# The steps of a long convolution, put on TensorE as row tiles and column tiles instead of zero-padded full-size products

## The chip, the cores and the metric

The kernel runs on one core of one Trainium2 chip. The metric is the device time of one execution in microseconds (us). The kernel before takes 2110.37 us, the median of three runs (2103.78 to 2110.42).

## The reference: what is computed

The program computes a layer and its gradients. The input is normalized over its 1024 channels, then goes into two branches: branch A, a long convolution along the 2048 positions for each channel, and branch B, a gated MLP of width 3584.

```
xn = layernorm(x)
# branch A: q = xn
k_shift[t] = sum over i<4 of k[t-i] * shift_k[i]          # four taps per channel
kv = k_shift * v
y  = irfft(rfft(kv, padded to 4096) * rfft(ssm_k, padded to 4096))[:2048] + kv * ssm_D
A  = xn * y
# branch B
h  = relu(xn @ W_gate) * (xn @ W_up);   B = h @ W_down
out = x + A + B
# then jax.vjp: the gradients of out for x, k, v, shift_k, ssm_k, ssm_D, W_gate, W_up, W_down
```

All tensors are bf16. The ten outputs are `out` and nine gradients.

## The kernel before, in words

**Branch B** (class `LnMlp`) is a chain of large matrix products of 128 x 128 weights by 512 columns: `hidden` (up, gate and the gradient of the hidden layer; L573), `grad_down` and `grad_in` (weight gradients; L670), then `out_phase` (L754) and `grad_x` (L787). ScalarE (ACT) and VectorE (DVE) take its results out of the accumulators, and all its stores and loads go through SyncE's queue (SP).

**Branch A** (class `ABranch`) works on eight groups of 128 channels, one after the other (`steps`). The 2048 positions are split in stages, so that each Fourier transform becomes small matrix products. For one group:

- `h_tile`: 16 transposes on TensorE turn the filter `ssm_k` so that positions lie on partitions (`pst`); DVE copies the result to `hT`.
- `fwd1` (three times: filter `hT`, gradient `gt`, signal `kvt`): four accumulators of two products each (weights `R`, 512 columns); ACT copies each to `B`; DVE's `flip` transposes `B` in blocks of 32.
- `fwd2` (three times): 32 products of 128 columns with the table `FW`; ACT writes `H`, `G`, `K`. `cmul` on DVE multiplies them pointwise.
- `inv_a` (three times) and `flip`: 32 products of 128 columns with the table `IA`.
- `inv_b` (for the gradient `gkv` and for `yt`): two accumulators of four products each with `RB`, 512 columns. `inv_b_chan` does the same for the gradient of the filter, with `RN`.
- `grad_taps`: 16 products of 512 columns accumulate, for every pair of channels in the group, the product of `gks` and `kp`; only the diagonal is used (DVE multiplies by the identity, `dg`, and sums).
- `gradients` on DVE: `gv`, `gks`, `gk`. A DMA `gks<-gks` copies the three first rows of each partition to the partition before, as the taps need them.

Before the change a partition holds 16 neighbouring positions (`tview`: partition q, row r). `R` has 128 rows, of which every second one is zero for each parity `u` of q; `RB` has 128 columns, of which every second one is zero for each `u`, and the two parities are summed in the accumulator.

**Order of the work.** Both branches are written as generators. Each `yield` of branch A gives a budget in nanoseconds, which the steps of branch B use up, so that steps of A are put between products of B. Every instruction carries a priority (`Pri.now`, or `Pri.late` for ACT, DVE and stores), and a planner then writes a fixed list for each engine by these priorities and by when it thinks that operands are ready. An engine works off its list in order. So the list of a queue, once written, decides who waits behind whom. Branch A has small pools: two accumulators (`aps`), three time tiles (`ts`), and one buffer each for `kp`, `vt` and `ksh` (`a_lng`): `kp` of the next group is loaded only when `grad_taps` of this group has read it.

Of the kernel before, what the change touches and what calls it, by code (L numbers as in the profile page):

```python
# [17 lines left out]
P = 128  # L18
# [21 lines left out]
NB1 = 32  # L40


class ABranch:

# [57 lines left out]
    def tables(self):  # L102
# [6 lines left out]
        self.R = con.tile([P, 2, 2, 2, NB1], BF16, name="R")  # L109
        self.RB = con.tile([P, 2, NB1, 2, 2], BF16, name="RB")  # L110
        self.RN = con.tile([P, NB1, 2], BF16, name="RN")
# [23 lines left out]
        n1 = pbit(124, 0.25, "n1p")  # L135
        nh = pbit(2, 0.5, "nhp")
        up = pbit(1, 1.0, "up")
# [10 lines left out]
        nu = lin(up, -1.0, 1.0, "nu")  # L148
        nnh = lin(nh, -1.0, 1.0, "nnh")
        for u, mu in ((0, nu), (1, up)):  # L150
            for n2h, mh in ((0, nnh), (1, nh)):
                V.tensor_scalar(out=self.R[:, u, n2h, :, :], in0=tr[:], scalar1=mu[:], scalar2=mh[:],
                                op0=ALU.mult, op1=ALU.mult)
# [42 lines left out]
        V.memset(self.RB[:], 0.0)  # L196
        nb64 = lin(b64, -1.0, 1.0, "nb64")
        for n2h, mh in ((0, nb64), (1, b64)):
            for o in (self.RB[:, 0, :, n2h, 0], self.RB[:, 1, :, n2h, 1], self.RN[:, :, n2h]):
                V.tensor_scalar(out=o, in0=trB[:], scalar1=mh[:], scalar2=1.0 / 2048, op0=ALU.mult, op1=ALU.mult)  # L200

        make_identity(nc, self.identA[:])
        sk_b = con.tile([P, self.NG * 4], BF16, name="sk_b")
# [8 lines left out]
    def tview(self, ap2d, cg):  # L212
        return ap2d[:, cg].rearrange("(q r) c -> q r c", r=16)
# [4 lines left out]
    def loads_1(self, gi):  # L218
# [4 lines left out]
        self.load(gt[:], self.tview(self.g, cg))  # L223
        xv = self.tview(self.xn_d, cg)
        xt = self.tmp.tile([P, 16, P], BF16, name="xt", tag="tmp")
        self.load(xt[:], xv)
# [5 lines left out]
    def loads_2(self, st):  # L232
# [8 lines left out]
        self.load(vt[:], self.tview(self.v, cg))  # L241
# [14 lines left out]
    def h_tile(self, st):  # L256
        hn = st["hn"]
        hT = self.ttile("hT")
        hv = hn[:].rearrange("p r c -> p (r c)").rearrange("p (q r) -> p r q", r=16)
        pst = self.ps.tile([P, 16, P], BF16, name="pst", tag="aps")  # L260
        for r in range(16):
            self.pri.now()
            self.nc.tensor.transpose(pst[:, r, :], hv[:, r, :], self.identA[:])
        self.vcopy(hT[:, 0:16, :], pst[:])
        return hT

    def flip(self, src):
# [3 lines left out]
        sf = src[:].rearrange("p cp r i -> p (cp r i)").bitcast(F32).rearrange("p (cp r) -> p cp r", cp=64)  # L271
# [5 lines left out]
    def fwd1(self, src, ns, add_D=None):  # L277
        B = self.big.tile([P, 64, NB1, 2], BF16, name="B", tag="big")
        for u in range(2):
            for j in range(2):  # L280
                ps = self.ps.tile([P, 1024], F32, name="ps1", tag="aps")
                for jj in range(2):
                    r0 = 8 * j + 4 * jj
                    self.mm(ps[:, 512 * jj:512 * jj + 512], self.R[:, u].rearrange("p h a k -> p (h a k)"),
                            src[:, r0:r0 + 4, :].rearrange("p r c -> p (r c)"))
                t0 = 16 * u + 8 * j
                self.act(B[:, :, t0:t0 + 8, :], ps[:].rearrange("p (r cp i) -> p cp r i", r=8, i=2))
                if add_D is not None and t0 == 0:
                    b0 = B[0:NB1, :, 0, :]
                    self.tt(b0, b0, add_D[:].rearrange("p (cp i) -> p cp i", i=2), ALU.add)  # L290
                if u + j == 2:
                    self.flipped = self.flip(B)
                yield ns
# [32 lines left out]
    def inv_a(self, Q, ns):  # L326
        C = self.big.tile([P, 64, NB1, 2], BF16, name="C", tag="big")
        for k0 in range(0, NB1, 8):
# [4 lines left out]
            if k0 == NB1 - 8:  # L333
                self.flipped = self.flip(C)
# [13 lines left out]
    def inv_b_chan(self, Cf, dst, ns):  # L348
        dv = dst[:, 0:16, :].rearrange("p r c -> p (r c)").rearrange("p (q n) -> p q n", n=NB1)
        for n0 in range(0, NB1, 16):  # L350
            ps = self.ps.tile([P, 16, 64], F32, name="ps5", tag="aps")
            for j in range(16):
                self.mm(ps[:, j, :], Cf[:, n0 + j, :], self.RN[:].rearrange("p n h -> p (n h)"))
# [3 lines left out]
    def grad_taps(self, gi, gks, kp, ns):  # L357

        ps = self.ps.tile([P, 4, P], F32, name="ps6", tag="aps")
        for r in range(16):  # L360
            self.mm(ps[:].rearrange("p b c -> p (b c)"), gks[:, r, :], kp[:, r:r + 4, :].rearrange("p b c -> p (b c)"),
                    start=(r == 0), stop=(r == 15))
            if r % 4 == 3:
                if r == 15:
                    dg = self.tmp.tile([P, 4, P], F32, name="dg", tag="tmp")
                    self.tt(dg[:], ps[:], self.identA[:].rearrange("p (o c) -> p o c", o=1).to_broadcast([P, 4, P]),
                            ALU.mult)
                    self.pri.late()
                    self.nc.vector.tensor_reduce(out=self.gs_all[:, gi, :], in_=dg[:], axis=AX.X, op=ALU.add)
                yield ns  # L370

    def steps(self):
# [4 lines left out]
        for gi in range(self.NG):  # L377
# [39 lines left out]
            self.store(self.tview(self.y_d, cg), yt[:, 0:16, :])  # L417
# [498 lines left out]
```

## Time and profile before

| what | before |
|---|---|
| median of three runs | 2110.37 us |
| the profiled execution's own time | 2113.93 us |
| its span | 2112.2 us |
| granted TensorE clock, mean | 0.978 |
| TensorE products (PE) busy | 1983.0 us, 94% |
| VectorE (DVE) busy | 1003.4 us, 48% |
| ScalarE (ACT) busy | 693.2 us, 33% |
| end of branch A's last products | about 1310 us from the start |

A row of a group reads: line, engine, operation, output<-inputs, shape and count, then busy us, mean ns of one, and the engine's idle time just before with what ended it. A row of the timeline reads: start, length, engine, line, operation, count, and in brackets the idle time before it and its releaser. A product's length in these rows reaches from its start to its modelled end; the spacing of products in a stream is shorter, and is read from two starts.

### The profile page before, as it was taken

To read this page: it belongs to the slowest core of one execution; us is meant where nothing else is said; L and a number is where in the kernel's file an instruction comes from. 1 tells how busy PE (TensorE), PEld (TensorE's weight loads), DVE (VectorE), ACT (ScalarE), POOL (GpSimd) and SP (SyncE) were. 2 spreads that over 40 slices of the span, in tenths; PEclk is the share of its full clock that TensorE was granted. 3 is DMA by queue.
4 is the path that set the end of the run, shared out by engine and by line. 5 is a ranking of instruction groups with operands and counts; after the bars stand their busy time and mean duration, and the time that the engine had idled before them with its cause. 6 is when DMAs were issued, how large, how long until landed. Compare 5 with 4: busy or idle time off the path is not lost.

```text
span 2112.2 us, 26202 instructions
## 1 busy us (share of the span) xinstructions
PE 1983.0 (94%) x10502; PEld 947.0 (45%) x10502; DVE 1003.4 (48%) x1450; ACT 693.2 (33%) x902; POOL 20.1 (1%) x46
## 2 busy tenths in 40 slices
PE   3799989889999998989999899999998999999998
PEld 2345435445444544535445454444443444444443
DVE  4848667666865954746557574000011213232232
ACT  6455337337436535537365373111100000000000
POOL 2000000000000000000000000000000000000000
PEclk9899999989999999999999999999998999999999
DMA  9764565965466474352473425933499745544551
GB/s 259 191 162 120 156 173 138 211 156 145 118 166 176 143 210 126 102 147 93 133 218 107 134 71 162 313 116 116 105 249 241 185 120 131 126 110 110 127 122 53
DMA packets 614811, 319.03 MB, mean 151 GB/s; under 512 B 448800, under 2 KB 583968, under 8 KB 614688
## 3 DMA queue, kind: packets, MB, share of 16 engines
q1 hardware_dynamic: 613408, 313.15, 55.7%
q0 software_dynamic: 1280, 4.20, 0.6%
q8 instruction: 82, 1.34, 0.3%
q14 instruction: 41, 0.34, 0.1%
HBM read 141.36 MB, written 95.44 MB: 112 GB/s over the span
## 4 chain that ended last, share of the span: by engine, by line
PE 78%; DVE 7%; DMA 7%; ACT 4%; issue 2%; SPq 1%; DVEq 0%; POOL 0%; ACTq 0%
PE ps_x L787 18%; PE ps_w L670 16%; PE ps_o L754 9%; PE ps L64 7%; PE ps_u L573 7%; PE ps_g L573 7%; PE ps_h L573 7%; PE ps_d L670 6%; DMA kp<-in_A_k_dram 3%; DVE tap L72 1%; ACT H L68 1%; ACT G L68 1%; DMA gks<-gks 1%; DVE ksh L72 1%; DVE flp L274 1%
## 5 line engine op out<-in xcount | busy, mean ns | idle before, releaser
L670 PE MATMUL ps_w<-ugs,xn_nat 128*128 128x512 bf16 x1792 | 403.0, 380 | 5.1 <-DMA xn_nat<-xn_d 5.1
L573 PEld LDWEIGHTS <-xnT 128*128 128x128 bf16 x1792 | 174.7, 99 | 210.4 <-issue 19.9
L670 PEld LDWEIGHTS <-xn_nat 128*128 128x128 bf16 x1792 | 173.4, 98 | 206.4 <-DMA xn_nat<-xn_d 5.8
L573 PE MATMUL ps_h<-wdT,goT 128*128 128x512 bf16 x896 | 213.7, 385 | 13.9 <-DVE ru L631 11.7
L573 PE MATMUL ps_g<-wg,xnT 128*128 128x512 bf16 x896 | 214.1, 389 | 5.4 <-DVE ru L631 5.4
L670 PE MATMUL ps_d<-g_nat,hs 128*128 128x512 bf16 x896 | 212.9, 386 | 4.0 <-DMA g_nat<-in_grad_out_dram 4.0
L573 PE MATMUL ps_u<-wu,xnT 128*128 128x512 bf16 x896 | 209.8, 381 | 1.4 <-DMA wu<-in_B_W_up_dram 1.2
L754 PE MATMUL ps_o<-wd,hT 128*128 128x512 bf16 x896 | 199.5, 387 | 8.0 <-DMA hT<-h_d 8.0
L787 PE MATMUL ps_x<-wuT,guT 128*128 128x512 bf16 x896 | 198.6, 379 | 0.0
L787 PE MATMUL ps_x<-wgT,ggT 128*128 128x512 bf16 x896 | 198.6, 379 | 0.0
L756 DVE TENSOR_TENSOR o<-ps_o,ya 128x512 bf16<-128x512 f32 x32 | 21.5, 687 | 263.5 <-PE ps_o L754 263.5
L754 PEld LDWEIGHTS <-hT 128*128 128x128 bf16 x896 | 88.9, 99 | 118.4 <-DMA hT<-h_d 9.2
L708 ACT CAST wi<-ps_w 128x512 bf16<-128x512 f32 x112 | 65.5, 586 | 229.8 <-PE ps_w L670 226.7
L643 ACT CAST gh<-ps_h 128x512 bf16<-128x512 f32 x112 | 65.5, 585 | 228.3 <-PE ps_h L573 119.4
L573 PEld LDWEIGHTS <-goT 128*128 128x128 bf16 x896 | 87.0, 99 | 113.5 <-issue 21.2
L787 PEld LDWEIGHTS <-ggT 128*128 128x128 bf16 x896 | 87.7, 98 | 105.7
L787 PEld LDWEIGHTS <-guT 128*128 128x128 bf16 x896 | 87.7, 98 | 105.7
L274 DVE STREAM_TRANSPOSE flp<-B 128x1024 f32<-128x1024 f32 x48 | 89.8, 1938 | 93.9 <-ACT B L68 93.9
L670 PEld LDWEIGHTS <-hs 128*128 128x128 bf16 x896 | 86.9, 99 | 103.4 <-issue 12.6
L789 DVE CUSTOM_DVE_ANT_0 gx<-ps_x,gy 128x512 f32<-128x512 f32 x32 | 22.1, 692 | 223.2 <-PE ps_x L787 223.2
L68 ACT CAST B<-ps 128x1024 bf16<-128x1024 f32 x96 | 96.2, 1016 | 76.5 <-PE ps L64 76.3
L68 ACT CAST C<-ps 128x1024 bf16<-128x1024 f32 x96 | 96.7, 1019 | 51.0 <-PE ps L64 51.0
(159 smaller groups left out, 1769.9 us busy)
## 6 DMA issues: line engine op xcount, KB each, us to landing
ug_d<-ru SPq DMA_DIRECT2D x112, 256.0 KB, 2.8
ugs<-ug_d SPq DMA_DIRECT2D x112, 256.0 KB, 4.8
wg<-in_B_W_gate_dram SPq DMA_DIRECT2D x56, 256.0 KB, 4.2
wu<-in_B_W_up_dram SPq DMA_DIRECT2D x56, 256.0 KB, 3.8
h_d<-ht SPq DMA_DIRECT2D x112, 128.0 KB, 2.0
hs<-h_d SPq DMA_DIRECT2D x56, 256.0 KB, 4.6
out_dram<-wi SPq DMA_DIRECT2D x56, 256.0 KB, 3.3
out_dram<-wo SPq DMA_DIRECT2D x28, 256.0 KB, 2.0
```

The costliest lines, as they stand in the source:

```text
L64: self.nc.tensor.matmul(out, lhsT=lhsT, rhs=rhs, start=start, stop=stop)
L68: self.nc.scalar.copy(out=out, in_=in_)
L72: self.nc.vector.tensor_tensor(out=out, in0=in0, in1=in1, op=op)
L274: self.nc.vector.transpose(out=df[:, c0:c0 + 32, :], in_=sf[:, c0:c0 + 32, :])
L573: self.nc.tensor.matmul(ps[:], lhsT=xT[:, kt * P:(kt + 1) * P], rhs=w(kt), start=(kt == 0), stop=(kt == self.DT - 1))
L643: nc.scalar.copy(out=gh[:], in_=ps[:])
L670: self.nc.tensor.matmul(ps[:], lhsT=lhsT(st), rhs=rhs(st), start=(st == 0), stop=(st == self.ST - 1))
L708: nc.scalar.copy(out=wo[:, d, :], in_=ps[:])
L754: nc.tensor.matmul(ps[:], lhsT=hT[:, kt, :], rhs=self.wd[:, kt, oc], start=(kt == 0), stop=(kt == self.FT - 1))
L756: nc.vector.tensor_tensor(out=o0[:, oc], in0=ps[:], in1=ya[:, oc], op=ALU.add)
L787: nc.tensor.matmul(ps[:], lhsT=T[:, kt, :], rhs=W[:, kt, oc], start=(i == 0), stop=(i == n - 1))
L789: V.tensor_tensor_reduce(out=gx[:, oc], in0=ps[:], in1=gy[:, oc], scale=1.0, scalar=0.0, op0=ALU.add, op1=ALU.add, accum_out=m[:, ob:ob + 1])
```

## The change

Positions are dealt out in another way: partition 64u + q holds row r of positions 32q + 16u + r, so that the parity `u` selects a half of the partitions. The padded zeros then go away:

- `fwd1`: `R` becomes a table of 64 rows for each half. A pair of products takes rows 0 to 63 and rows 64 to 127, each into its own 512-column half of the accumulator (two row tiles). There are as many products as before.
- `inv_b`: `RB` becomes 64 columns. The two products of a parity pair no longer accumulate; they write partitions 0 to 63 and 64 to 127 (two column tiles). There are as many products as before.
- `grad_taps`: each of the 16 products of 128 x 128 by 512 becomes four products of 32 channels by their own 32 channels and 4 shifts (128 columns) into four column tiles. 64 products in place of 16; the two DVE steps behind read 128 columns in place of 512. The generator yields once in place of four times.
- `h_tile`: each transpose becomes two with 64 columns of weights.
- Every load and store of a time tile is two DMAs of 64 partitions; so are the loads of `kp`'s three extra rows and the copy `gks<-gks`.

```diff
     def tview(self, ap2d, cg):
-        return ap2d[:, cg].rearrange("(q r) c -> q r c", r=16)
+        return ap2d[:, cg].rearrange("(q u r) c -> u q r c", u=2, r=16)
+
+    def load_time(self, t, ap2d, cg):
+        for u in range(2):
+            self.load(t[64 * u:64 * u + 64], self.tview(ap2d, cg)[u])
+
+    def store_time(self, ap2d, cg, t):
+        for u in range(2):
+            self.store(self.tview(ap2d, cg)[u], t[64 * u:64 * u + 64, 0:16, :])
...
-        self.load(kp[:, 3:19, :], kv)
-        self.load(kp[1:P, 0:3, :], kv[0:P - 1, 13:16, :])
+        self.load_time(kp[:, 3:19, :], self.k, cg)
+        self.load(kp[64:P, 0:3, :], kv[0, :, 13:16, :])
+        self.load(kp[1:64, 0:3, :], kv[1, 0:63, 13:16, :])
...
         for r in range(16):
-            self.pri.now()
-            self.nc.tensor.transpose(pst[:, r, :], hv[:, r, :], self.identA[:])
+            for u in range(2):
+                self.pri.now()
+                self.nc.tensor.transpose(pst[64 * u:64 * u + 64, r, :], hv[:, r, u, :], self.identA[:])
...
     def fwd1(self, src, ns, add_D=None):
...
+        for r0 in range(0, 16, 4):
+            ps = self.ps.tile([P, 2, 4, P], F32, name="ps1", tag="aps")
+            for u in range(2):
+                rows = slice(64 * u, 64 * u + 64)
+                self.mm(ps[:, u].rearrange("p r c -> p (r c)"), self.R[rows].rearrange("p h a k -> p (h a k)"),
+                        src[rows, r0:r0 + 4, :].rearrange("p r c -> p (r c)"))
+            self.act(B[:, :, :, r0:r0 + 4, :], ps[:].rearrange("p u r (cp i) -> p cp u r i", i=2))
...
     def inv_b(self, Cf, dst, ns):
...
-                    self.mm(ps[:, 512 * jj:512 * jj + 512], self.RB[:, u].rearrange("p n h u -> p (n h u)"),
-                            Cf[:, n0:n0 + 4, :].rearrange("p n c -> p (n c)"), start=u == 0, stop=u == 1)
+                    self.mm(ps[64 * u:64 * u + 64, 512 * jj:512 * jj + 512],
+                            self.RB[:].rearrange("p n h -> p (n h)"), Cf[:, n0:n0 + 4, :].rearrange("p n c -> p (n c)"))
...
     def grad_taps(self, gi, gks, kp, ns):
 
-        ps = self.ps.tile([P, 4, P], F32, name="ps6", tag="aps")
+        ps = self.ps.tile([P, 4, 32], F32, name="ps6", tag="aps")
         for r in range(16):
...
+            for b in range(0, P, 32):
+                self.mm(ps[b:b + 32], gks[:, r, b:b + 32], kp[:, r:r + 4, b:b + 32], start=(r == 0), stop=(r == 15))
+        dg = self.tmp.tile([P, 4, 32], F32, name="dg", tag="tmp")
+        self.tt(dg[:], ps[:], self.ident32[:].to_broadcast([P, 4, 32]), ALU.mult)
...
-        self.store(gks[0:P - 1, 16:19, :], gks[1:P, 0:3, :])
+        self.store(gks[0:64, 16:19, :], gks[64:P, 0:3, :])
+        self.store(gks[64:P - 1, 16:19, :], gks[1:64, 0:3, :])
```

**What moves in the lists.** The planner writes other lists, because tiles, DMAs and budgets have changed. Two places show it, both at the passage from the fifth group of channels to the sixth (call such a passage a seam; there are seven).

DVE before, at the end of the fifth group: `ksh<-kp` is the first step that reads the next group's `kp`, and `hT<-pst` is the copy that the next group's first `fwd1` reads.

```order
L72 TENSOR_TENSOR dg<-ps_8301,identA 128x512
L369 TENSOR_REDUCE gs_all<-dg 128x4
L76 COPY gD_all<-ghn 128x1
L72 TENSOR_TENSOR ksh<-kp,skb 128x2048
L72 TENSOR_TENSOR tap<-kp,skb 128x2048 x2
L72 TENSOR_TENSOR ksh<-ksh,tap 128x2048 x2
L76 COPY hT<-pst 128x2048
```

DVE in the changed kernel, at the same place:

```order
L73 TENSOR_TENSOR dg<-ps_8499,ident_443 128x128
L371 TENSOR_REDUCE gs_all<-dg 128x4
L77 COPY gD_all<-ghn 128x1
L77 COPY hT<-pst 128x2048
L73 TENSOR_TENSOR ksh<-kp,skb 128x2048
L73 TENSOR_TENSOR B<-B,sD 32x64x2
L73 TENSOR_TENSOR tap<-kp,skb 128x2048 x2
```

The copy to `hT` has moved ahead of the steps that read `kp`. It stands behind them in all seven seams before, and ahead of them in four of the seven now (first to second group, fourth to fifth, fifth to sixth, seventh to eighth).

SP before, at the same seam: `kp` is loaded by two DMAs that stand behind the store of `gk`, the result of DVE's last taps.

```order
L84 DMA gks<-gks 127x384
L84 DMA y_d<-yt 2048x1x128
L691 DMA out_dram<-wo 128x1024
L80 DMA skb<-sk_d 128x512
L84 DMA out_dram<-gk 2048x1x128
L80 DMA kp<-in_A_k_dram 128x16x128
L80 DMA kp<-in_A_k_dram 127x3x128
```

SP in the changed kernel:

```order
L85 DMA gks<-gks 64x384
L85 DMA gks<-gks 63x384
L694 DMA out_dram<-wo 128x1024
L85 DMA y_d<-yt 64x16x128
L85 DMA y_d<-yt 64x16x128
L81 DMA kp<-in_A_k_dram 64x16x128
L81 DMA kp<-in_A_k_dram 64x16x128
L81 DMA kp<-in_A_k_dram 64x3x128
L81 DMA kp<-in_A_k_dram 63x3x128
L81 DMA skb<-sk_d 128x512
```

The loads of `kp` have moved ahead of `skb` and of the store of `gk`, and the whole program has 72 more DMAs on SP (1084 against 1012).

On PE the tiled products stand between full-size ones. In the changed list there are 135 runs of tiled products (88 of row tiles in `fwd1`, 39 of 64-column tiles in `inv_b` and `h_tile`, 8 of 32-column tiles in `grad_taps`), so TensorE goes 270 times from one kind of product to the other. The 64 products of `grad_taps` stand in one run; before, its 16 stood in three or four runs with products of branch B between them. At the fifth seam 50 products of branch B now stand between `inv_b` and the third `inv_a`, where 8 stood; and 1 or 2 stand between the four tiles of that `inv_a`, where none or 8 stood.

More of the change, by code (lines that the diff above doesn't have):

```diff
@@ L277, in fwd1 @@
     def fwd1(self, src, ns, add_D=None):
[L278 to L293, printed above, removed]
+        B = self.big.tile([P, 64, 2, 16, 2], BF16, name="B", tag="big")
+        for r0 in range(0, 16, 4):
[5 more added lines that the diff above has]
+            self.act(B[:, :, :, r0:r0 + 4, :], ps[:].rearrange("p u r (cp i) -> p cp u r i", i=2))
+            if add_D is not None and r0 == 0:
+                b0 = B[0:NB1, :, 0, 0, :]
+                self.tt(b0, b0, add_D[:].rearrange("p (cp i) -> p cp i", i=2), ALU.add)
+            if r0 == 12:
+                self.flipped = self.flip(B[:].rearrange("p cp u r i -> p cp (u r) i"))
+            yield ns
     def fwd2(self, Bf, F, ns):
@@ L357, in grad_taps @@
     def grad_taps(self, gi, gks, kp, ns):
-        ps = self.ps.tile([P, 4, P], F32, name="ps6", tag="aps")
+        ps = self.ps.tile([P, 4, 32], F32, name="ps6", tag="aps")
         for r in range(16):
[L361 to L370, printed above, removed]
+            for b in range(0, P, 32):
+                self.mm(ps[b:b + 32], gks[:, r, b:b + 32], kp[:, r:r + 4, b:b + 32], start=(r == 0), stop=(r == 15))
+        dg = self.tmp.tile([P, 4, 32], F32, name="dg", tag="tmp")
+        self.tt(dg[:], ps[:], self.ident32[:].to_broadcast([P, 4, 32]), ALU.mult)
+        self.pri.late()
+        self.nc.vector.tensor_reduce(out=self.gs_all[:, gi, :], in_=dg[:], axis=AX.X, op=ALU.add)
+        yield ns
     def steps(self):
```

45 lines of the change are left out of this document (20 added, 25 removed).

## The prediction

> **What bounds the kernel now.** I read the page first, then the groups of TensorE, the waits of PE, and the timeline at the places where PE waits.
>
> ```profile
> span 2112.2 us, 26202 instructions
> PE 1983.0 (94%) x10502; PEld 947.0 (45%) x10502; DVE 1003.4 (48%) x1450; ACT 693.2 (33%) x902; POOL 20.1 (1%) x46
> PE 78%; DVE 7%; DMA 7%; ACT 4%; issue 2%; SPq 1%; DVEq 0%; POOL 0%; ACTq 0%
> ```
>
> PE is busy 94% of the span and holds 78% of the chain that ended last. Both other shares matter: while branch A runs, DVE and DMAs are links of that chain. So there are two places for a gain or a loss: the time that PE needs for branch A's products, and PE's waits at the seams between groups. Time taken from PE shortens the end almost one for one, since branch B's products follow at once on the same engine.
>
> The products that the change touches, and two ACT groups that empty accumulators:
>
> ```profile
> L64 PE MATMUL ps<-hT,R 128*128 128x512 bf16 x64 | 22.7, 440 | 34.7 <-DVE hT L76 34.7
> L64 PE MATMUL ps<-kvt,R 128*128 128x512 bf16 x64 | 18.9, 379 | 1.4 <-ACT H L68 1.4
> L64 PE MATMUL ps<-gt,R 128*128 128x512 bf16 x64 | 18.7, 379 | 0.0
> L64 PE MATMUL ps<-flp,RB 128*128 128x512 bf16 x128 | 32.7, 379 | 1.8 <-ACT C L68 1.8
> L64 PE MATMUL ps<-kp,gks 128*128 128x512 bf16 x128 | 32.2, 379 | 0.0
> L263 PE MATMUL pst<-identA,hn 128*128 128x128 bf16 x128 | 10.6, 236 | 0.0
> L64 PEld LDWEIGHTS <-RB 128*128 128x128 bf16 x128 | 12.5, 98 | 17.1 <-issue 2.1
> L68 ACT CAST C<-ps 128x1024 bf16<-128x1024 f32 x96 | 96.7, 1019 | 51.0 <-PE ps L64 51.0
> ```
>
> The busy sums hold each short run's last tail and are not what a product costs in a stream. That is read from starts:
>
> ```profile
> 95.35 3.62 PE L573 MATMUL ps_h<-wdT,goT 128*128 128x512 bf16 x16
> 98.80 3.62 PE L573 MATMUL ps_g<-wg,xnT 128*128 128x512 bf16 x16
> 303.99 0.59 PE L64 MATMUL ps<-gt,R 128*128 128x512 bf16 x2
> 304.42 1.89 PE L573 MATMUL ps_g<-wg,xnT 128*128 128x512 bf16 x8
> 314.35 0.61 PE L64 MATMUL ps<-flp,FW 128*128 128x128 bf16 x8
> 314.80 1.89 PE L573 MATMUL ps_h<-wdT,goT 128*128 128x512 bf16 x8
> 265.94 0.64 PE L64 MATMUL ps<-RN,flp 128*128 128x64 bf16 x16 [0.85 <-DVE flp L274]
> 266.41 1.89 PE L573 MATMUL ps_h<-wdT,goT 128*128 128x512 bf16 x8
> 925.17 1.16 PE L263 MATMUL pst<-identA,hn 128*128 128x128 bf16 x16
> 926.16 2.54 PE L670 MATMUL ps_d<-g_nat,hs 128*128 128x512 bf16 x11
> ```
>
> Sixteen products of 512 columns take 98.80 - 95.35 = 3.45 us, 216 ns each. A pair of `fwd1` takes 0.43 us, twice that: a pair of A between products of B costs nothing beside its columns. Eight products of 128 columns take 0.45 us, 56 ns each, sixteen of 64 columns 0.47 us, 29 ns each, sixteen transposes 0.99 us, 62 ns each; in all of them the weight load (98 ns) hides.
>
> **The tiles, term by term.**
>
> *fwd1.* 3 x 64 products in 96 pairs. If the halves run side by side, one of two costs nothing: 96 x 0.216 = -20.7 us. If they run one after the other, 0. *inv_b.* 128 products in 64 pairs: -13.8 us, or 0. *grad_taps.* 128 products cost 27.6 us. They become 512 of 128 columns in 128 sets of four. One set at full overlap is one product, 56 ns (sum 7.2); one after the other, 512 x 56 ns = 28.7. Between them lies the shortest spacing that any pair of load and product shows, 29 ns: four of these are 0.118 us a set, 15.0 us. I take that row, because a set still brings four loads and four products: -12.6 us. *h_tile.* 128 transposes cost 7.9 us; 256 cost between 7.4 (29 ns each) and 15.9 (62 ns each). I take the middle, 45 ns, 11.5 us: +3.6 us. Together -43.5 us if tiles run side by side. I take side by side, as the halves use other rows or other columns of the array; no row of before shows two products at once, so the other end stays a rival.
>
> *Switches.* 270 times TensorE goes from full-size to tiled products or back. No row shows such a switch. At the least it costs nothing; at the most the next product waits until the last one has ended, 379 - 216 = 163 ns behind its usual start, and its load is not hidden either, 98 ns more: 261 ns, 70.5 us in all. I take 100 ns, because the nearest row is the tail of 163 ns and part of a tail is reading and writing that need not keep the next product away: +27.0 us. This eats `fwd1`'s gain nearly whole: a pair saves 216 ns and is mostly alone between two switches, 200 ns. The sure gains are the long runs of `grad_taps`.
>
> The Trainium skill (TensorEngine Tiling (Array Packing), Key Properties) says that a change of tiling mode drains TensorE, though not for how long; with the tail alone as the drain the switches would be 44.0 us, and the tiles would bring +0.5 us in place of -16.5. No run here shows which it is.
>
> Tiles in sum: -43.5 + 27.0 = -16.5 us.
>
> **The seams.** PE's largest wait in branch A is for `hT`:
>
> ```profile
> PE ps L64 <- DVE hT L76: 34.7, 6, 9.6
> PE ps L64 <- ACT yt L68: 7.7, 2, 6.5
> ```
>
> The fifth seam shows why, on PE, SP and DVE:
>
> ```profile
> 912.74 3.62 PE L670 MATMUL ps_d<-g_nat,hs 128*128 128x512 bf16 x16
> 938.27 1.03 PE L64 MATMUL ps<-hT,R 128*128 128x512 bf16 x2 [9.56 <-DVE hT L76]
> 939.09 2.34 PE L670 MATMUL ps_d<-g_nat,hs 128*128 128x512 bf16 x5
> 941.23 1.06 PE L64 MATMUL ps<-hT,R 128*128 128x512 bf16 x2
> 942.08 2.67 PE L670 MATMUL ps_d<-g_nat,hs 128*128 128x512 bf16 x8
> 944.59 0.59 PE L64 MATMUL ps<-hT,R 128*128 128x512 bf16 x2
> 918.35 0.58 SPq L84 DMA_DIRECT2D out_dram<-gk  x1
> 919.01 3.31 SPq L80 DMA_DIRECT2D kp<-in_A_k_dram  x2
> 931.18 1.23 DVE L72 TENSOR_TENSOR ksh<-kp,skb 128x2048 bf16<-128x2048 bf16 x1 [11.49 <-DMA kp<-in_A_k_dram]
> 936.99 1.22 DVE L76 COPY hT<-pst 128x2048 bf16<-128x2048 bf16 x1
> ```
>
> The last taps of `grad_taps` have started by 912.74, so `kp` is free about then. Its load is issued at 919.01, after the store of `gk`, and lands when DVE starts `ksh` at 931.18. The transposes for `hT` were done at 926.2, but the copy stands behind `ksh` and its taps until 936.99. PE stands still for 9.56 us, and then runs slowly: its next 2 + 5 + 2 + 8 = 17 products take 944.59 - 938.27 = 6.32 us in place of 17 x 0.216 = 3.67 us, 2.65 us more. The other seams where the copy now goes first:
>
> ```profile
> 285.81 3.57 PE L573 MATMUL ps_g<-wg,xnT 128*128 128x512 bf16 x8 [5.18 <-DVE ru L631]
> 292.22 1.01 PE L64 MATMUL ps<-hT,R 128*128 128x512 bf16 x2 [2.84 <-DVE hT L76]
> 804.91 1.03 PE L64 MATMUL ps<-hT,R 128*128 128x512 bf16 x2 [6.85 <-DVE hT L76]
> 1193.59 1.89 PE L64 MATMUL ps<-hT,R 128*128 128x512 bf16 x4 [7.71 <-DVE hT L76]
> 423.22 1.01 PE L64 MATMUL ps<-GH,IA 128*128 128x128 bf16 x8 [6.53 <-ACT yt L68]
> ```
>
> Waits at these four seams: 5.18 + 2.84 + 6.85 + 9.56 + 7.71 = 32.1 us, and 4 x 2.65 = 10.6 us of slow products: 42.7 us. In the changed lists the copy does not wait for `kp`, and `kp` is loaded some 6 us sooner (919.01 - 912.74), since SP no longer waits for `gk` first. That is a gain which the tiles have nothing to do with. It is not whole, for what was late is late elsewhere: DVE still stands at `ksh` until `kp` has landed (12.2 us after its issue at the fifth seam), now in four DMAs in place of two, and behind it stand `B`'s addition and flips, which `fwd2` needs, and while `hidden` runs the steps `ru` that free branch B's accumulators. And the seam is shorter in products of B, so that any late DMA shows on PE sooner. The best end is -49.2 us (all of it, and the wait of 6.53 us before `GH`, in front of which 50 products of B now stand at the fifth seam in place of 8). The worst is a loss of some 9 us: four tiles of the third `inv_a` follow one another at 0.45 + 0.43 = 0.88 us, but ACT needs 1.02 us to empty one, 0.14 us x 3 x 8 = 3.4 us, and one late wait like the 5.18 us above. I take half of 42.7: -21.4 us.
>
> **At nothing.** The smaller `dg` and its sum save DVE some microseconds in eight places where PE waits for something else. ACT empties as many accumulators of the same size (1.02 us each). 72 more DMAs on SP at some 0.58 us (the store of `gk` above) are 42 us of SP's time over 1200 us; they hide behind SP's idle time except at the seams, where they are in the half above. Branch A ends sooner in the list, but what follows it, `grad_in` and the last two phases, is PE's own work and is not shortened.
>
> **The sum.** The profiled execution took 2113.9 us, 1.7 us more than its span. 2113.9 - 16.5 - 21.4 = 2076.0 us; it lies 3.6 us above the median of the runs shown, so I predict 2072 us for the median. The forecast's own range is 2052 to 2093 (20 us each way: 75 ns more or less for each switch).
>
> **The rivals.**
>
> *The weight loads come out of hiding (slower).* Column tiles of `inv_b`, `grad_taps` and `h_tile` share all their rows with the product before, and 128 + 512 + 256 = 896 loads might have to wait for it. At 98 ns each this is 88 us: -43.5 + 27.0 + 88 - 21.4 = +50, 2160 us. It decides from (16.5 + 21.4) / 896 = 42 ns a load on. Against it: the eight products of 128 columns at 56 ns above, whose loads of 98 ns lie under products on the same rows. For it: none of those rows is of a tiled product.
>
> The Trainium skill (TensorE: Matmul & The Clock Gate, Part 3: Packing small matmuls) states this rule, that a load overlaps a running product only where their row groups differ, and in its column example still reports 2.38 times for three column tiles; the 56 ns spacing of this trace does not agree with it for full-size products.
>
> *The tiles run one after the other (the change does not do what it says).* `fwd1` and `inv_b` save nothing, `grad_taps` costs 1.1 us more, `h_tile` at worst 8.0, the switches 27.0: +36.1 - 21.4 = +14.7, 2125 us. For it: no row shows two products at once.
>
> *The seams give nothing back.* DVE's wait at `ksh` reaches PE by another way. Only the tiles remain: 2110.4 - 16.5 = 2094 us. For it: the wait of 5.18 us for `ru` came by that way.
>
> *Free switches.* -43.5 - 21.4 = -64.9: 2045 us. For it: today's pair of A costs exactly its columns. *Free switches and clean seams:* -43.5 - 42.7 = -86.2: 2024 us.
>
> **How the numbers follow.** Forecast 0.45; loads exposed 0.12; one after the other 0.07; seams give nothing 0.14; free switches 0.14; both best 0.08. The range 2036 to 2118 leaves out the last, and the two slower ones: the first of these wholly, the second in its upper part. A measurement of this kernel tells a change from none at about 0.3%, 6.3 us. Faster: 0.44 of the forecast, 0.11 of the seams' case, 0.22 of the best two, less a little for what I have not seen in lists that moved so far, 0.74. Same 0.08 (the tails between). Slower 0.18.
>
> **What would show it.** Two products of a pair starting within some tens of ns of each other would show tiles side by side; starts 216 ns apart would show the contrary. The gap from the last full-size product to the first tiled one, against 216 ns, is the switch. In `grad_taps` one run of 64 in about 1.9 us is the forecast, 3.6 us is one after the other, 10 us is exposed loads. For the seams: PE's wait for `hT` falls from 34.7 us to under 10, and `kp` is issued within 1 to 2 us of the last tap. I am wrong if PE waits in new places for ACT or DMAs by more than 40 us in branch A's time, or if a switch costs over 240 ns.

## The result, and the profile after

The changed kernel takes 2039.15 us, the median of four runs (2038.72 to 2040.87); the kernel before takes 2108.26 us beside it. The ratio is 0.9676, with a 95% interval of 0.9657 to 0.9696: 69 us faster. The forecast was 2072 us. The direction is right and the time lies inside the range, but the point is 33 us too high, so one of its terms must be far off.

The head of the page of the changed kernel, and its row in the view of the cores (the row before reads `2112.2 us, clock 0.978`):

```profile
span 2037.0 us, 27072 instructions
PE 1930.9 (95%) x10806; PEld 914.7 (45%) x11014; DVE 995.2 (49%) x1444; ACT 690.4 (34%) x902; POOL 20.1 (1%) x46
```

```profile
core 0: 2037.0 us, clock 0.992
```

The profiled span fell by 75.2 us. Both kinds of loss shrank: PE is busy for less time, and the clock that TensorE was granted went up. In both traces the clock's records hold only full clock and half clock. Half clock was granted for 93.3 us before and for 32.3 us after, but PE worked in only 59.4 us and 18.0 us of that; in the rest it stood still anyway. Counting half of the time in which PE worked as lost, I estimate 29.7 us lost before and 9.0 us after, 20.7 us less. The mean clock alone would give (1 - 0.978) x 2112 = 46.5 us and (1 - 0.992) x 2037 = 16.3 us, because it counts the idle stretches too. The fifth seam before shows both cases:

```profile
core 0: us, PE busy (x) PEld busy (x) DVE busy (x) ACT busy (x) POOL busy (x), PEclk, DMA share, GB/s
933.40:938.27 4.87, 0.00 (x1) 0.01 (x1) 4.84 (x6) 0.00 (x0) 0.00 (x0) 0.50 0.03 13
938.27:943.60 5.33, 5.33 (x13) 1.93 (x14) 3.60 (x4) 2.02 (x2) 0.00 (x0) 0.50 0.80 197
```

The clock is at 0.50 in both stretches. In the first PE waits for `hT` and loses nothing by it; in the second it loses 5.33 / 2 = 2.67 us, the 2.65 us of slow products that the prediction had found there.

The trace after lacks some records of products: its page counts 10806 products and 11014 weight loads, where the page before counts 10502 of each and every product has its own load. So PE's busy time after is somewhat understated, and some gaps in its timeline are none.

The changed groups, from the view of groups with shapes kept apart:

```profile
L65 PE MATMUL ps<-hT,R 64*128 64x512 bf16 x64 | 12.0, 384 | 0.6
L65 PE MATMUL ps<-gt,R 64*128 64x512 bf16 x64 | 12.3, 385 | 0.1
L65 PE MATMUL ps<-flp,RB 128*64 128x512 bf16 x128 | 19.7, 391 | 0.3
L65 PE MATMUL ps<-kp,gks 128*32 128x128 bf16 x512 | 8.6, 220 | 0.1
L270 PE MATMUL pst<-identA,hn 128*64 128x128 bf16 x256 | 16.0, 280 | 0.3 <-ACT ghn L69 0.3
L270 PEld LDWEIGHTS <-hn 128*64 128x64 bf16 x256 | 15.2, 204 | 4.0 <-issue 3.8 <-PE ps L65 0.2
```

PE's idle time before `ps<-hT,R` was 34.7 us and is 0.6 us. Busy time fell everywhere but in the transposes, which went from 10.6 us to 16.0 us.

PE's waits in branch A's time:

```profile
PE ps L65 <- DVE flp L281: 17.1, 9, 2.9
PE ps L65 <- ACT H L69: 6.0, 7, 2.0
```

The wait for `hT` has left the list. Two smaller ones are larger: PE now waits 17.1 us (before 1.8) for DVE's flips, nearly all of it ahead of `inv_b_chan`, and 6.0 us (before 2.1) for ACT's copies to `H`. All of PE's listed waits together went from 120.5 us to 86.3 us. Of the latter 2.9 us are put down to issue, in gaps of up to 0.2 us such as a missing record leaves; without them 83.4 us remain, 37.1 us less than before.

**What a tile costs.** PE's timeline of the changed kernel, around a pair of `fwd1`, a tile of `inv_b`, and the fifth seam:

```profile
117.70 1.90 PE L576 MATMUL ps_g<-wg,xnT 128*128 128x512 bf16 x8
119.53 0.39 PE L65 MATMUL ps<-hT,R 64*128 64x512 bf16 x2
119.85 1.47 PE L576 MATMUL ps_u<-wu,xnT 128*128 128x512 bf16 x6
...
220.06 1.90 PE L576 MATMUL ps_h<-wdT,goT 128*128 128x512 bf16 x8
221.89 0.62 PE L65 MATMUL ps<-flp,RB 128*64 128x512 bf16 x4
222.45 0.82 PE L576 MATMUL ps_h<-wdT,goT 128*128 128x512 bf16 x3
...
846.46 0.60 PE L673 MATMUL ps_d<-g_nat,hs 128*128 128x512 bf16 x2
847.03 1.08 PE L65 MATMUL ps<-kp,gks 128*32 128x128 bf16 x64
848.27 3.40 PE L673 MATMUL ps_d<-g_nat,hs 128*128 128x512 bf16 x15 [0.16 <-issue]
...
855.25 1.99 PE L270 MATMUL pst<-identA,hn 128*64 128x128 bf16 x32
857.18 1.90 PE L673 MATMUL ps_d<-g_nat,hs 128*128 128x512 bf16 x8
859.01 0.39 PE L65 MATMUL ps<-hT,R 64*128 64x512 bf16 x2
```

Two row tiles of 0.38 us each end within 0.39 us of the first one's start, so they run side by side; their starts lie 2 to 6 ns apart. Eight full-size products take 8 x 0.216 = 1.73 us; the first tile should start at 117.70 + 1.73 = 119.43 and starts at 119.53: the switch costs 0.10 us. From 119.53 to the next full-size product are 0.32 us, 0.216 for the pair and 0.10 for the way back. Between the full-size products the visit took 119.85 - 119.43 = 0.42 us, and before it took 0.43 us. That visit has gained next to nothing.

The 0.16 us of "issue" behind the run of taps is a missing record. The weight loads of the stream that follows begin sooner, and there are 16 of them to 15 products:

```profile
848.04 3.14 PEld L673 LDWEIGHTS <-hs 128*128 128x128 bf16 x16
```

The same gap stands behind all eight runs of taps in this trace and makes the visit look 1.37 us long. In runs 9 to 11, whose traces have as many products as loads, most visits take 1.14 us, and that is the figure taken here.

The same reckoning for the visits of the four kinds gives the whole account of the tiles (medians; in `h_tile` the gaps are left out):

| visit | before, us | after, us | visits | sum | forecast with its switches |
|---|---|---|---|---|---|
| pair of `fwd1` | 0.432 | 0.418 | 96 | -1.3 | -3.1 (176 switches) |
| tile of `inv_b` | 0.863 | 0.649 | 32 | -6.8 | |
| `grad_taps` | 3.45 | 1.14 | 8 | -18.5 | -11.0 (16 switches) |
| `h_tile` | 0.99 | 2.09 | 8 | +8.8 | |
| all | | | | -17.8 | -16.5 |

`inv_b` and `h_tile` share 78 switches in the forecast: -13.8 + 3.6 + 7.8 = -2.4 us, against -6.8 + 8.8 = +2.0 us measured. The sum of the tiles agrees with the forecast to 1.3 us, but by luck: `grad_taps` came out 7.5 us better, `inv_b` with `h_tile` 4.4 us worse and `fwd1` 1.8 us worse. The three parts, tiles 17.8, listed waits 37.1 and products at half clock 20.7, come to 75.6 us; the span fell by 75.2 us.

**The fifth seam, on DVE and SP:**

```profile
857.29 1.23 DVE L77 COPY hT<-pst 128x2048 bf16<-128x2048 bf16 x1 [2.66 <-PE pst L270]
858.43 1.22 DVE L73 TENSOR_TENSOR ksh<-kp,skb 128x2048 bf16<-128x2048 bf16 x1
848.15 2.65 SPq L81 DMA_DIRECT2D kp<-in_A_k_dram  x4
876.01 1.24 SPq L85 DMA_DIRECT2D out_dram<-gk  x1
```

`kp` is issued at 848.15, when the run of taps ends (847.03 + 1.08 = 848.11), and 28 us ahead of the store of `gk`. The copy to `hT` follows its transposes at once, and `ksh` right behind it has no wait for `kp`. Before, the copy stood 11.8 us behind the start of the transposes (936.99 - 925.17); here it is 2.0 us (857.29 - 855.25).

### The profile page after: what moved, and what is told of

The parts are those of the page before. It is cut to its first block, busy times and chain, and to the rows that moved or that the text cites. A ratio compares the mean times of both kernels' runs of the same rounds, so it can differ in the third digit from the quotient of the medians.

```text
span 2037.0 us, 27072 instructions
## 1 busy us (share of the span) xinstructions
PE 1930.9 (95%) x10806; PEld 914.7 (45%) x11014; DVE 995.2 (49%) x1444; ACT 690.4 (34%) x902; POOL 20.1 (1%) x46
## 5 line engine op out<-in xcount | busy, mean ns | idle before, releaser
L673 PE MATMUL ps_w<-ugs,xn_nat 128*128 128x512 bf16 x1746 | 395.3, 380 | 2.7 <-issue 0.5
L576 PEld LDWEIGHTS <-xnT 128*128 128x128 bf16 x1792 | 169.3, 98 | 201.2 <-issue 18.7
L576 PE MATMUL ps_h<-wdT,goT 128*128 128x512 bf16 x865 | 205.7, 382 | 13.4 <-DVE ru L634 11.4
L576 PE MATMUL ps_g<-wg,xnT 128*128 128x512 bf16 x875 | 207.8, 383 | 4.2 <-DVE ru L634 2.6
L576 PE MATMUL ps_u<-wu,xnT 128*128 128x512 bf16 x870 | 205.6, 380 | 1.7 <-issue 0.5
L673 PE MATMUL ps_d<-g_nat,hs 128*128 128x512 bf16 x866 | 203.1, 380 | 4.1 <-DMA ug_d<-ru 1.4
L757 PE MATMUL ps_o<-wd,hT 128*128 128x512 bf16 x878 | 195.0, 382 | 9.8 <-DMA hT<-h_d 8.9
L673 PEld LDWEIGHTS <-hs 128*128 128x128 bf16 x896 | 82.6, 98 | 98.7 <-issue 9.1
L634 DVE SCALAR_TENSOR_TENSOR ru<-ru,ps_u 128x512 bf16<-128x512 bf16 x112 | 76.0, 680 | 73.8 <-PE ps_u L576 47.9
```

Of the source, the lines that this page charges most:

```text
L576: self.nc.tensor.matmul(ps[:], lhsT=xT[:, kt * P:(kt + 1) * P], rhs=w(kt), start=(kt == 0), stop=(kt == self.DT - 1))
L634: nc.vector.scalar_tensor_tensor(out=ru[s][:, 1, :], in0=ru[s][:, 0, :], scalar=0.0, in1=ps[:], op0=ALU.is_gt, op1=ALU.mult)
L673: self.nc.tensor.matmul(ps[:], lhsT=lhsT(st), rhs=rhs(st), start=(st == 0), stop=(st == self.ST - 1))
L757: nc.tensor.matmul(ps[:], lhsT=hT[:, kt, :], rhs=self.wd[:, kt, oc], start=(kt == 0), stop=(kt == self.FT - 1))
```

## The experiments

Theory A: most of the gain comes from the seams, that is from the lists that the planner wrote anew, and the tiles bring little. It was later split: A1, the copy to `hT` had to move ahead of `ksh`; A2, it is enough that `kp` is loaded early. The rivals stand in each expectation. Every kernel was timed beside the kernel before, whose median was 2107.5 to 2108.3 us throughout.

### 1. The copy to hT on another engine (kernel before)

```diff
-        self.vcopy(hT[:, 0:16, :], pst[:])
+        self.act(hT[:, 0:16, :], pst[:])
```

> The kernel before, with one edit: ScalarE instead of VectorE copies the turned filter to hT. The lists of the engines stay otherwise as they were. Theory A (the gain came mostly from the seams: the copy to hT stood behind steps that wait for kp): PE's wait for hT falls from 34.7 us to under 8, the slow products behind it go too (about 6 x 2.65 us), and 30 to 45 us of the time are gone: 2063 to 2078 us. Rival B (the gain came from the products on TensorE, the seams only moved): within 6 us of before, since VectorE still stands at ksh until kp has landed and holds up PE by another way.

Measured 2066.38 us, ratio 0.9799 (0.9784 to 0.9814): 42 us faster with no tile and no new layout. Its waits of DVE and PE:

```profile
DVE ksh L72 <- DMA kp<-in_A_k_dram: 55.0, 7, 11.4
PE ps L64 <- ACT hT L68: 5.7, 1, 5.7
```

DVE stands at `ksh` for `kp` as long as before (before: `DVE ksh L72 <- DMA kp<-in_A_k_dram: 56.5, 7, 11.5`), and PE pays for it no longer: the 5.7 us are one wait ahead of the first group, at no seam. The clock rose to 0.990. So DVE's wait does little harm in itself here; it cost time because the copy was queued behind it. That takes away the main reason for which the prediction halved the gain of the seams.

### 2 and 3. One yield, and the 32-column tiles alone (kernel before)

```diff
-            if r % 4 == 3:
-                ...
-                yield ns
+        yield ns
```

The second kernel has this and the four 32-column tiles of `grad_taps`, and nothing else of the change.

> The kernel before, with one edit: grad_taps gives its budget once instead of four times (same full-size products). The copy to hT stays behind ksh in six of the seven seams, and the seams come closer together. Theory A: no gain, 2100 to 2118 us. Rival C (the smaller budget of branch A is what shortened the program): at least 20 us less, 2088 us or under.

> The kernel before with only grad_taps in 32-column tiles, and its budget given once; lists nearly those of one_yield. Both theories: against one_yield the difference is what the tiles of grad_taps bring. In the changed kernel a visit of 64 tiled products takes 1.37 us with both switches where 16 full-size ones took 3.45 us, so 8 x 2.08 = 16.6 us less than one_yield: 2084 to 2101 us. If tiles bring their gain only together with the other lists: no difference from one_yield.

One yield: 2118.63 us, 1.0047 (1.0032 to 1.0062), slower by 10 us and just above the range expected for no gain. The tiles of `grad_taps` alone: 2114.32 us, 1.0032 (1.0020 to 1.0043), 4 us less, which the two intervals don't tell from nothing. The visit itself shrank as it should (3.45 us before; now 1.33 us in a trace that again lacks a product's record behind it, so about 1.1 us), but PE's waits show where it went, first with one yield, then with the tiles too:

```profile
PE ps L64 <- DVE flp L274: 28.8, 8, 7.3
PE ps L64 <- DVE hT L76: 31.4, 7, 8.7
```

```profile
PE ps L64 <- DVE flp L277: 38.6, 8, 8.4
PE ps L64 <- DVE hT L76: 22.9, 7, 5.0
```

The flips ahead of `inv_b_chan` are not finished any sooner when PE arrives sooner (38.6 us of this wait in place of 28.8 us). Time saved on PE in front of a wait for DVE becomes a longer wait. The expected 16.6 us was a miss; what came is the other case named there, no difference.

### 4. The new layout with full-size products (changed kernel)

The changed kernel with zero-padded full-size tables in `fwd1` and `inv_b`, and the full `grad_taps` with four yields; the doubled DMAs and the transposes in halves stay.

```diff
-                self.mm(ps[:, u]..., self.R[rows]..., src[rows, r0:r0 + 4, :]...)
+                self.mm(ps[:, u]..., self.R[:, u]..., src[:, r0:r0 + 4, :]...)
```

> The changed kernel with full-size products, padded with zeros, in fwd1, inv_b and grad_taps (budget given four times there); the new order of positions, the doubled DMAs and the 64-column transposes of h_tile stay. The copy to hT stands ahead of ksh in three of the seven seams, and kp is loaded ahead of the store of gk in most. Theory A (tiles bring about 16 us, of which the transposes cost 8.7; the seams about 58): the products of before plus 8.7 us, and a good half of the seams' gain: 2065 to 2095 us. Rival B: 2110 us or more, for without tiles nothing is gained.

Measured 2050.13 us, 0.9717 (0.9701 to 0.9734): 58 of the 69 us without the tiles of `fwd1`, `inv_b` and `grad_taps`, and with the dearer transposes in it; that is more than theory A had said (2065 to 2095 us). PE's waits for DVE:

```profile
PE ps L65 <- DVE flp L286: 2.2, 2, 1.6
PE ps L65 <- DVE hT L77: 1.3, 1, 1.3
```

The seams are clean here. The three kinds of tiles should then bring 1.3 + 6.8 + 18.5 = 26.6 us more, and the changed kernel is only 11 us faster than this one: 17.1 - 2.2 = 14.9 us are in the longer wait for flips. This kernel holds the new lists, the new order of positions and the halved DMAs together. That the smaller DMAs bring `kp` sooner by themselves was not tried; run 1, which has none of them, shows 42 us of the gain without.

### 5. The copy made to depend on kp (changed kernel)

```diff
-        self.vcopy(hT[:, 0:16, :], pst[:])
+        self.pri.late()
+        self.nc.vector.scalar_tensor_tensor(out=hT[:, 0:16, :], in0=st["kp"][:, 3:19, :], scalar=0.0,
+                                            in1=pst[:], op0=ALU.mult, op1=ALU.add)
```

> The changed kernel, with the copy to hT made to read kp as well (times zero), so that it waits for kp to land as before the change; kp is still loaded early. Two theories of the seams. A1 (it was the place of the copy): PE's wait for hT comes back, 4 to 8 us a seam with slow products behind it, 30 to 60 us more than the changed kernel: 2069 to 2099 us. A2 (it was the load of kp, issued within 2 us of the last tap instead of 6 us after): kp has landed by the time the copy is due, and the cost is the copy's own and some 1 to 2 us a seam: 2042 to 2060 us.

Measured 2044.45 us, 0.9698 (0.9673 to 0.9723), 5 us more than the changed kernel. At the fifth seam the step still waits for the transposes and not for `kp`:

```profile
861.21 2.29 DVE L272 SCALAR_TENSOR_TENSOR hT<-kp,pst 128x2048 bf16<-128x2048 bf16 x1 [2.66 <-PE pst L270]
```

I read this as A2: `kp` has landed in time, so the copy needn't come first. But the copy kept its place ahead of `ksh` here, and in six of the seven seams of this list 4 to 13 more products of B stand ahead of `fwd1`. The 5 us themselves are not told from nothing, as the intervals of the two kernels overlap. Run 12 puts A2 to the test.

### 6 to 8. The filter in full-size products; the old budget (changed kernel)

Run 6 takes the filter's part back: 16 full transposes in place of 32 halves, and a padded table for the filter's `fwd1`. Run 7 gives `grad_taps` the budget of four yields. Run 8 has both.

```diff
-            for u in range(2):
-                self.nc.tensor.transpose(pst[64 * u:64 * u + 64, r, :], hv[:, r, u, :], self.identA[:])
+            self.nc.tensor.transpose(pst[:, r, :], hv[:, r, :], self.identA[:])
...
-        yield ns
+        yield 4 * ns
```

> The changed kernel, with the filter's part put back: 16 full-size transposes per group in the old order of positions, and full-size products with the padded table in its fwd1 (one third of the row tiles). In the changed kernel a visit of 32 tiled transposes takes 2.08 us where 16 full-size ones took 0.99 us, and a pair of fwd1 takes 0.42 us against 0.43. So 8 x 1.09 = 8.7 us less and 0.3 us more: 2028 to 2035 us. If the transposes' longer visit only fills time in which PE would have waited for VectorE's copy: no difference from 2039 us.

> The changed kernel, with grad_taps giving four times the budget at its one yield, so that branch A gets as many products of branch B between its steps as before. Theory: the changed kernel's wait for the flips before inv_b_chan (17.1 us) comes from seams that are too short in products of B; they get longer, the wait falls under 6 us, the kernel takes 2024 to 2033 us. Rival: branch A ends later and loses as much at the seams that stay short, 2036 to 2045 us.

> Both edits, of filter_full and of budget4, in one kernel. If they add up: 8.7 us and some 11 us less than the changed kernel, 2014 to 2027 us.

Measured 2037.14 us (0.9662, 0.9635 to 0.9689), 2036.52 us (0.9660, 0.9637 to 0.9684) and 2029.69 us (0.9622, 0.9596 to 0.9649). Alone each gives 2 to 3 us, which the intervals don't tell from nothing and which is below what was expected; for run 7 that is the rival's range. Together they give 9.5 us, also less than expected (2014 to 2027 us). The transposes did get shorter (a visit of about 1.2 us in place of 2.09). With the filter in full size the wait for flips stays:

```profile
PE ps L65 <- DVE flp L299: 16.7, 9, 3.3
```

With the old budget alone it is 12.8 us, with both edits 13.3 us, where under 6 us was expected. A budget of four yields given at once is too small to cover the flips.

### 9 to 11. Fewer switches; branch B spread over the seams

Run 9 lets the changed kernel yield after every second accumulator of `fwd1`, so that there are 60 runs of row tiles in place of 88. Run 10 is run 8 with slower paces for branch A, so that more products of B stand in it. Run 11 has both.

```diff
-            yield ns
+            if r0 % 8 == 4:
+                yield 2 * ns
...
-        yield 0.9, b.hidden(...)
-        yield 1.3, b.grad_down(...)
-        yield 1.3, b.grad_in(...)
+        yield 0.78, b.hidden(...)
+        yield 1.13, b.grad_down(...)
+        yield 1.13, b.grad_in(...)
```

> The changed kernel, with fwd1 yielding once after every two accumulators, so that 60 runs of row tiles stand in the list in place of 88 (two pairs in one run). If a switch costs 0.1 us each way and pairs run side by side (visits of 2 products 0.42 us, of 4 products 0.63 us in the changed kernel's trace): 28 x 0.21 = 5.9 us less, 2030 to 2036 us. Rival: both accumulators of branch A are then full at once and TensorE waits for ScalarE instead, 2038 us or more.

> The kernel filter_full_budget4 with branch A spread over more of branch B (pace 0.78 and 1.13 in place of 0.9 and 1.3). Theory: its 13.3 us of waiting for the flips before inv_b_chan come from too few products of B in the seams; with more of them most goes: 2014 to 2024 us. Rival: the copy to hT stands behind ksh in six of the seven seams here, and the waits for it come back: 2035 us or more. If an early load of kp is enough, it does not matter.

> Both edits, of spread and of pairs_joined (78 runs of tiled products in place of 104): 26 x 0.21 = 5.5 us less than spread.

Joined pairs: 2039.93 us, 0.9678 (0.9665 to 0.9692), no gain, as the rival had it. The visits of four products take 0.633 us as expected, but PE then waits longer for ACT to empty two accumulators in a row (6.0 us before the edit):

```profile
PE ps L65 <- ACT H L69: 10.6, 12, 2.3
```

Spread: 2017.69 us, 0.9572 (0.9559 to 0.9585), as expected, and better than both kernels by far more than the intervals. The waits for flips and `hT`:

```profile
PE ps L65 <- DVE flp L299: 4.0, 3, 1.9
PE ps L65 <- DVE hT L77: 2.1, 1, 2.1
```

In six of the seven seams of this list the copy stands behind `ksh`, and PE still waits only 2.1 us for it: the place of the copy does not decide alone.

Both together: 2017.30 us, 0.9573 (0.9560 to 0.9586), nothing on top; 5.5 us were expected.

### 12. kp loaded first, everything else old (kernel before)

```diff
-        self.load(kp[1:P, 0:3, :], kv[0:P - 1, 13:16, :])
+        self.pri.now()
+        self.kp_dma = nc.sync.dma_start(out=kp[1:P, 0:3, :], in_=kv[0:P - 1, 13:16, :])
...
+        with self.tc.issue_after(self.kp_dma.ins):
+            self.load(skb[:]...)
...
+            with self.tc.issue_after(self.kp_dma.ins):
+                self.store(self.tview(self.out_gk, cg), self.gk[:, 0:16, :])
```

> The kernel before, with one thing changed on SP: in every seam the two loads of kp stand ahead of skb and of the store of gk (the loads wait for grad_taps alone, and skb and the store are queued behind them). Old layout, full-size products, four pieces of grad_taps; the copy to hT stays behind ksh in all seven seams. Theory A2 (the early load of kp is what gives the gain): at the fifth seam of the kernel before, kp could be issued some 6 us sooner (919.01 - 912.74) and DVE would then be late by 3 to 4 us in place of 9.56. PE's wait for hT falls from 34.7 us to under 12, DVE's wait at ksh from 56.5 us to under 25, and with the slow products gone the time is 2065 to 2085 us (before 2108). Rival: in the old layout the load lands late in any case, or the copy behind ksh makes PE wait as before: the wait for hT stays over 25 us and the time is 2095 to 2110 us; then what the changed kernel gains in its seams needs its other new places too.

Measured 2099.29 us, 0.9959 (0.9946 to 0.9971): 9 us less, inside the rival's range, and A2 falls as a cause that is enough by itself. Waits, and the fifth seam on DVE and SP:

```profile
DVE ksh L72 <- DMA skb<-sk_d: 49.5, 7, 8.5
PE ps L64 <- DVE hT L76: 26.9, 6, 6.4
```

```profile
910.14 1.21 DVE L72 TENSOR_TENSOR tap<-gks,skb 128x2048 bf16<-128x2048 bf16 x1
920.24 1.23 DVE L72 TENSOR_TENSOR ksh<-kp,skb 128x2048 bf16<-128x2048 bf16 x1 [4.64 <-DMA skb<-sk_d]
928.45 1.22 DVE L76 COPY hT<-pst 128x2048 bf16<-128x2048 bf16 x1
908.85 0.57 SPq L80 DMA_DIRECT2D kp<-in_A_k_dram  x1
911.37 5.90 SPq L80 DMA_DIRECT2D skb<-sk_d  x1
```

`kp` is issued at 908.85, and at once the next link holds the seam: `skb` has one buffer, which DVE's last tap of `gk` reads until 910.14 + 1.21 = 911.35; its load is issued at 911.37, and DVE gets it at 920.24. Then `ksh` and its taps still stand ahead of the copy, 928.45 - 920.24 = 8.2 us of DVE's work. Three links lie ahead of the copy, and taking one away leaves the others.

What differs between a seam that stalls and one that doesn't is the time between the transposes and the copy, against the products of B that stand before `fwd1`. Worked out from the timelines of PE and DVE: before, the six stalling seams have 8 to 16 products there (1.7 to 3.5 us), and the copy starts 4 to 13 us after the start of the transposes. In the changed kernel it starts 2 to 3 us after that in six of seven seams, behind 7 to 15 products. In the seventh, the passage from the sixth group to the seventh, it stands behind `ksh` as before and starts 12 us after it (971.27 to 983.02), but there 59 products of B stand ahead of `fwd1`:

```profile
971.27 1.99 PE L270 MATMUL pst<-identA,hn 128*64 128x128 bf16 x32 [0.26 <-ACT ghn L69]
973.19 13.12 PE L673 MATMUL ps_d<-g_nat,hs 128*128 128x512 bf16 x59
986.25 0.61 PE L65 MATMUL ps<-hT,R 64*128 64x512 bf16 x4
```

So the old lists disagreed: PE's had `fwd1` close behind the transposes, while DVE's had the copy behind a load and some 8 us of taps. Each change seen here that brings the two together took the wait away: another engine for the copy (run 1), the copy ahead of `ksh` or `ksh` ready sooner (the changed kernel, runs 4 and 5), or more of B between (this seam).

## Why the prediction was right or wrong

**What bounds the kernel: right.** The two places named, the time of A's products and the seams, are where the gain arose: 17.8 us in the tiles, and 37.1 + 20.7 = 57.8 us in waits and in products at half clock.

**fwd1, -20.7 us less its switches: right.** The halves run side by side, and the two switches of a lone pair eat the gain: -1.3 us measured, -3.1 us forecast.

**The switches, 100 ns: right, though no row of before decided between 0 and 261 ns, so the hit was partly luck.** Most entries measure 0.093 to 0.097 us, and the way back 0.095 to 0.103 us. Where only one to three full-size products stand ahead, some entries take longer, 0.13 to 0.35 us; why is not shown. The Trainium skill (TensorEngine Tiling (Array Packing), Key Properties) says that a change of tiling mode drains TensorE. The trace agrees that a change costs time, 0.10 us each way, less than the 0.163 us tail that I had tried as the drain.

**inv_b, -13.8 us: right** (0.649 us for four products is two pairs of 0.216 us, two switches of about 0.10 us and 0.02 us more).

**grad_taps, "four of these are 0.118 us a set": too slow.** The run of 64 products takes 1.08 us to the modelled end of the last one, which is 0.22 us long, so its 64 starts lie (1.08 - 0.22) / 63 = 13.7 ns apart: 55 ns a set, one product of 128 columns (56 ns). Full overlap was the end that I had not taken. With switches that is 7.5 us better than the forecast.

**h_tile, "I take the middle, 45 ns": too fast.** 32 half transposes take (857.18 - 855.25) / 32 = 60 ns each with the way back, as long as the full ones (62 ns). They do not run side by side: +8.8 us with their switches, against +3.6 us and some 1.6 us of switches. That it is their weight loads that hold them (204 ns against 150 ns for the full ones) was not tried.

**The seams, "I take half of 42.7: -21.4 us": this step failed, and it is nearly the whole error of the point.** The mechanism was named rightly, the size not: waits and products at half clock fell by 57.8 us, 36.4 us more than forecast, and the profiled execution took 2038.7 us, 37.3 us less than the sum of 2076.0. Run 4, with clean seams and without three of the four kinds of tiles, gained 58 us, and run 1 gained 42 us by the copy alone. Three things were off. First, next to nothing came back by way of `ksh`: DVE's wait there could last 55.0 us without a wait of PE for `hT` at any seam (run 1). Second, the sum held four seams and had left out others that kept the copy behind `ksh` in the list; there `ksh` was ready sooner, and their waits went too, as did the one of 6.53 us for `yt` that stood only in the best end. Third, slow products were counted as 4 x 2.65 = 10.6 us, while 20.7 us of them went. What I should have seen in the trace of before: PE works in 59.4 us at half clock, so slow products cost some 29.7 us, far more than four short runs explain.

**At nothing: partly wrong.** Of the doubled DMAs no wait shows on branch A's products. But the single yield of `grad_taps` has no term of its own, only the words "any late DMA shows on PE sooner", and with it came the longer wait for flips, 17.1 us. One yield alone raised this wait from 1.8 us to 28.8 us (run 2), and it is DVE's flips that are late there, not a DMA.

**The rivals.** Loads coming out of hiding fell: four column tiles a set, with 97 ns for a load, take 55 ns a set.

```profile
L65 PEld LDWEIGHTS <-gks 128*32 128x32 bf16 x512 | 7.4, 97 | 3.4 <-issue 1.7 <-ACT C L69 1.3 <-DVE gk L73 0.4
```

The Trainium skill (TensorE: Matmul & The Clock Gate, Part 3: Packing small matmuls) holds that a load overlaps a running product only where the row groups differ; these share all rows and their loads hide all the same, so the trace does not agree. Tiles one after the other fell for three of four kinds and held for the transposes. "The seams give nothing back" fell to runs 1 and 4. The rival whose number came closest, free switches at 2045 us, was wrong in its mechanism: the switches are not free, it was the seams that were clean. Forecast switches with clean seams would have been 2113.9 - 16.5 - 42.7 = 2054.7 us, 16 us above the profiled execution; 20.7 - 10.6 = 10.1 us of that are slow products.

**What would show it.** The pair side by side, the wait for `hT` under 10 us and `kp` within 1 to 2 us of the last tap came as written; the run of taps took 1.08 us, less than the forecast's 1.9. No sign named the transposes, which gained nothing, or DVE's flips, which came too late.

## What to carry to other kernels

A pair of half-array tiles between full-size products saves one product's time and pays for two switches, which here leaves 0.01 us; tiles pay in long runs, as in `grad_taps`. When a change makes a planner write its lists anew, compare how far apart producer and consumer stand on their two engines at the places where the bound engine waits today; that can be worth more than the edited arithmetic, and it can be tried alone, by moving one copy to another engine. Time saved ahead of a wait for another engine only lengthens that wait, so look there next. Price a stall on TensorE with the slow products behind it, and count half clock only where TensorE works. Before a small gap is read as a wait, compare the counts of products and of weight loads.

## What the runs showed of the hardware

- Row tiles of 64 and column tiles of 64 run two at a time, 32-column tiles four at a time at 55 ns a set; transposes into 64-column tiles run one at a time, about 60 ns each.
- A change between full-size and tiled products costs about 0.10 us, in either direction.
- The granted clock was lower where the seams stall: 0.975 to 0.982 before and in runs 2, 3 and 12, and 0.988 to 0.993 in the changed kernel and the other runs. At the fifth seam before, half clock set in during the stall and lasted into the products behind it.
